# Sparse attention with a squared-ReLU FFN on one core: queries and choices transposed together by DMA

## The chip, the cores and the metric

The kernel runs on one core of one Trainium2 chip. The metric is the device time of one execution in microseconds, taken over several runs. A core has five engines that run their own instruction queues: TensorE (PE: matmuls, and transposes as matmuls with an identity), VectorE (DVE), ScalarE (ACT), GpSimd (POOL) and SyncE (SP), which only issues DMAs here. [...] Matmuls write PSUM; VectorE and ScalarE bring results from there to SBUF.

## What is computed

Attention over batch 4, 8 heads, 768 positions of 64 dimensions, in which each query looks at the 6 best of its chunks of 32 keys, followed by an FFN over the 3072 tokens with a squared ReLU. Cut to what matters:

```python
k_chunks = k.reshape(B, H, nc, chunk, D)            # chunk 32, nc 24
k_min, k_max = np.min(k_chunks, axis=3), np.max(k_chunks, axis=3)
ub = np.sum(np.maximum(q[:, :, :, None, :] * k_min[:, :, None, :, :],
                       q[:, :, :, None, :] * k_max[:, :, None, :, :]), axis=-1)
ub = np.where(causal, ub, -1000000000.0)            # by chunk
top_chunks = np.argsort(ub, axis=-1)[..., -top_k:]  # top_k 6
scores = scale * np.matmul(q, k.transpose(0, 1, 3, 2))
mask = sel & (pos[:, None] >= pos[None, :])         # sel: key's chunk is chosen
scores = np.where(mask, scores, -1000000000.0)
attn = np.exp(scores - np.max(scores, axis=-1, keepdims=True))
attn = attn / (np.sum(attn, axis=-1, keepdims=True) + 1e-09)
x = np.matmul(attn, v)                              # (B, S, H * D) = 3072 x 512
h = np.maximum(x @ w_in, 0.0)                       # 512 -> 2048
out = h * h @ w_out                                 # 2048 -> 512
```

## The kernel before

The work is cut into 8 half-blocks: half a batch, 384 queries, in the order `ORDER` (b0 first half, b1 first half, b0 second, b1 second, then b2 and b3, first half and second). A half-block has 4 slots `p`, one for each pair of heads; the 32 slots `s` run one after the other, and slot `s` is `p = s % 4` of half-block `hb = s // 4`. A first half (half 0) attends to 384 keys, a second half (half 1) to 768.

A slot's steps are written out by hand in one loop (a manual schedule: each engine executes its instructions in the order of the program text):

- `step_P`: the pair's keys and queries come with dimensions on the partitions. For the first three half-blocks TensorE transposes them (`step_T`) and they are placed in `kqs`; from half-block 3 (`ON_PE = 3`) on, DMA transposes bring a whole half-block (`tr`, one DMA of 4 blocks of 128x128 for each 128 tokens of k or q, into `kqT`), and `place_dma` copies keys and queries from there to `kqs`. `relus` makes relu(-q) and relu(q), `qr`.
- `step_K` (in six parts `k1`, one half-block ahead) or `extrema`: minimum and maximum of each chunk of keys, spread into `kbds`.
- `step_U`: TensorE makes the bounds `ub` of each query and chunk, VectorE takes the 8 best (`nc.vector.max`, six or four of them) and writes 1 for each chunk that is not chosen into `nsel`.
- `step_V`: TensorE transposes `nsel` (2 or 3 transposes a pair, one per 128 queries; L391), VectorE copies the result into `kqs` for each head (L395, L396).
- `step_E(s, hh, n)`: scores of one head. The matmul's operand in `kqs` has 128 rows: 64 dimensions of the head, and 64 rows of codes. On the key side a code row is -2^24 in the keys of one chunk (`oneh`), on the query side it is the transposed `nsel`: a chunk that is not chosen gets a score that exp turns to 0. Heads have the two groups of rows the other way round (`QROW`, `SROW`). ScalarE takes exp (L414), POOL masks the diagonal blocks (`affine_select`, L418) for `n == 1`. The scores have 3 PSUM buffers.
- `step_F(s)`, one slot later: attention times v, whose 65th column is 1 and gives the sum; VectorE divides (L443, L444) and writes `x`. At the end of a half-block, `step_X` transposes `x` to `xT`: on TensorE with `x_T` for the first two half-blocks and the last, by three DMA transposes (L484) for the others. Then the FFN of that half-block is queued.

The FFN is filler for TensorE. `fill` (in the loop `f1`) takes one piece from `queue`: an up-projection `ffn_up` (4 matmuls of 384 columns into `ph`, two buffers; ScalarE's relu, VectorE's square to `h`) or a quarter of a down-projection `ffn_down` (4 matmuls of 512 columns into `py`, one buffer; after the fourth quarter a copy to `ob` and a store by SP, L546 and L550). `quota` limits a slot to 6 to 8 pieces. The small uses of `psA` (`ub`, `qt`, `po` and others, tag "att") share two PSUM buffers.

Loads go out on POOL's queue (they convert to bf16), stores and DMA transposes on SP's. They are hung onto slots: `at(s, ...)` fills `later[s]`, and `go(s, 2)` and `go(s, 99)` issue two and then all of them, the first between the scores of head 0, the second behind `step_V`. `first[s]` is issued at a slot's start. k and q of half-block `g >= 4` load in slots `4g - 6` and `4g - 5`, are transposed in `4g - 5` and `4g - 3` and placed in `4g - 2`.

Of the kernel before, what the change touches and what calls it, by code (L numbers as in the profile page):

```python
# [39 lines left out]
def kernel(  # L40
# [30 lines left out]
    QROW = (D, 0)  # L71
    SROW = (0, D)

    kqs = [consts.tile([128, 2, NP, 4, HB], BF16, tag=f"kq{i}", name="kq") for i in range(2)]


    qn0 = consts.tile([128, HT, NP, 4, D], BF16, tag="qn0", name="qn")
# [3 lines left out]
    nsel = [consts.tile([128, HT, 2, D], BF16, tag=f"ns{i}", name="nsel") for i in range(3)]  # L81
# [28 lines left out]
    def load_q0(h):  # L110
        nc.gpsimd.dma_start(
            out=qn0[:, :, h // 2, 1 + h % 2, :],
            in_=q[0, h, 0:HB].rearrange("(j p) d -> p j d", p=128))
# [39 lines left out]
    for h in (6, 7):  # L153
        load_q0(h)

    oneh = consts.tile([D, S], BF16, tag="oneh")
    nc.vector.tensor_scalar_mul(
        oneh.rearrange("p (c j) -> p c j", j=CH),
        ident[0:D, 0:NC].unsqueeze(2).to_broadcast([D, NC, CH]), OFFSEL)

    def codes(i, half, copy, p0=0, p1=NP):
        for h in range(2):
            copy(kqs[i][SROW[h]:SROW[h] + D, h, p0:p1, 2 * half, :],
                 oneh[:, HB * half:HB * half + HB].unsqueeze(1)
                 .to_broadcast([D, p1 - p0, HB]))
# [22 lines left out]
    def blank(p0, p1, c):  # L188

        nc.scalar.mul(qn0[:, :, p0:p1, c, :],  # L190
                      ident[:, 0:D].unsqueeze(1).unsqueeze(1)
                      .to_broadcast([128, HT, p1 - p0, D]), 0.0)

    def clear():

        for h in range(2):
            nc.vector.memset(kqs[1][SROW[h]:SROW[h] + D, h, :, 1, 0:128], 0.0)
# [32 lines left out]
    def step_cast(n, p):  # L230
        if n == "k":
            nc.vector.tensor_copy(packed("k", 0)[:, 2 * p:2 * p + 2], staged["k", p])
        else:
            nc.scalar.copy(qn0[:, :, p, 1:3, :], staged["q", p])

    def step_T(s, kp, qp, ns="kq"):
# [3 lines left out]
        for n in ns:  # L240
            pool, tag = kp if n == "k" else qp
            x = t[n] = pool.tile([128, HB], BF16, tag=tag, name="t" + n)
            if n == "q" and s < NP:
                for j in range(HT):
                    nc.tensor.matmul(
                        x[:, 128 * j:128 * (j + 1)],
                        lhsT=qn0[:, j, p, 1:3, :].rearrange("p h d -> p (h d)"),
                        rhs=ident, is_transpose=True, start=True, stop=True)
# [26 lines left out]
    def place(s, n, copy, h0=0, h1=2):  # L275
        b, half, p = slots[s]
        for h in range(h0, h1):
            copy(by_token(kqs[b % 2][QROW[h]:QROW[h] + D, h, p, 2 * half + "kq".index(n), :]),
# [9 lines left out]
    def place_dma(g):  # L288
        b, half = ORDER[g]
        for h in range(2):  # L290
            nc.sync.dma_start(
                out=kqs[b % 2][QROW[h]:QROW[h] + D, h, :, 2 * half:2 * half + 2, :],
                in_=half_T(g)[D * h:D * h + D])
# [53 lines left out]
    def step_U(s):  # L347
        b, half, p = slots[s]
        ncs = 12 * (half + 1)
# [11 lines left out]
        for j in range(j0, HT):  # L361
# [3 lines left out]
            (qn0[:, j0:, p, 0:4:3, 0:ncs] if s < NP else nsel[s % 3][:, j0:, :, 0:ncs]),  # L365
# [3 lines left out]
    def qc(s, h):  # L369
        b, half, p = slots[s]  # L370
        return kqs[b % 2][:, h, p, 2 * half + 1, :]

    def step_V(s):
        b, half, p = slots[s]
        st[s]["e"] = [None, None]
        if s < NP:
            qt = psA.tile([128, 2, HB], BF16, tag="att", name="qt")
            for hh in range(2):
                for j in range(HT):
                    nc.tensor.matmul(  # L380
                        qt[:, hh, 128 * j:128 * (j + 1)],
                        lhsT=qn0[:, j, p, 2 * hh:2 * hh + 2, :]
                        .rearrange("p h d -> p (h d)"),
                        rhs=ident, is_transpose=True, start=True, stop=True)
            nc.vector.tensor_copy(kqs[b % 2][:, :, p, 2 * half + 1, :], qt)
# [4 lines left out]
        for j in range(j0, HT):  # L390
            nc.tensor.matmul(  # L391
                qt[:, 128 * j:128 * (j + 1)],
                lhsT=nsel[s % 3][:, j].rearrange("p h d -> p (h d)"),
                rhs=ident, is_transpose=True, start=True, stop=True)
        nc.vector.tensor_copy(qc(s, 0)[0:D, c:], qt[0:D, c:])  # L395
        nc.vector.tensor_copy(  # L396
            qc(s, 1)[D:128, c:], qt[D:128, c:])

    def step_E(s, hh, n):
# [7 lines left out]
        for (at, j, i0, m) in BANKS[half][n]:  # L407
# [3 lines left out]
                lhsT=kqs[b % 2][:, hh, p, 2 * (j // HT), 128 * (j % HT):128 * (j % HT + 1)],  # L411
# [12 lines left out]
    def step_F(s, hh):  # L424
# [13 lines left out]
        if hh == 1:  # L438
            if p == 0:
                xs[s // NP] = work.tile([128, HT, DM], BF16, tag="x", name="x")  # L440
# [4 lines left out]
                x[:, :, 128 * p:128 * (p + 1)].rearrange("p j (h d) -> p h j d", h=2),  # L445
                po[:, :, :, 0:D], r.to_broadcast([128, 2, HT, D]))
            st.pop(s)
# [14 lines left out]
    def x_T(hb, g, pt, us=(0, 1)):  # L462
# [3 lines left out]
        for u in us:  # L466
            for j in range(HT):
                nc.tensor.matmul(
                    pts[hb, g][:, u, 128 * j:128 * (j + 1)],
                    lhsT=xs[hb][:, j, 128 * (2 * g + u):128 * (2 * g + u + 1)],  # L470
# [5 lines left out]
    def step_X(hb, pe):  # L476
        xT = xT_of(hb)
# [4 lines left out]
        else:  # L482
            for j in range(HT):
                nc.sync.dma_start_transpose(  # L484
                    out=xT[:, :, 128 * j:128 * (j + 1)], in_=xs[hb][:, j, :])
# [17 lines left out]
    def ffn_last(hb):  # L503
# [3 lines left out]
        for g in range(2):  # L507
# [5 lines left out]
            ob = late.tile([128, DM], F32, tag="ob", bufs=3, name="ob")  # L513
            for c in range(2):
                (nc.scalar.copy if c else nc.vector.tensor_copy)(
                    ob[:, 128 * c:128 * c + 128], y[:, 128 * c:128 * c + 128])
                (nc.scalar if c else nc.sync).dma_start(
                    out[r0:r0 + 128, w * g + 128 * c:w * g + 128 * c + 128],
                    ob[:, 128 * c:128 * c + 128])
# [13 lines left out]
    def ffn_down(hb, py, t, c, act, tail):  # L533
# [9 lines left out]
        if c == 3:  # L543
            ob = late.tile([128, DM], F32, tag="ob", bufs=3, name="ob")
# [46 lines left out]
    for b in range(2, B):  # L591
        for g in range(2):
            at(8 * b - 2 + g, load_v, b, 4 * g, 4 * g + 4)
    for g in range(4, 2 * B):
        for i in range(2 * HT):
            at(4 * g - 6 + i // HT, load_n, "kq"[i // HT], g, i % HT)
    for g in range(ON_PE, 2 * B):
        s0 = 4 * g - 4 + (g == ON_PE)
        if g == ON_PE:
            for i in range(2 * HT):  # L600
# [225 lines left out]
```

## Time and profile before

| | |
|---|---|
| median of 3 runs | 278.2 us (277.95 to 281.56) |
| the profiled execution | 278.13 us, of which the span from the first to the last instruction is 276.4 us |
| granted TensorE clock, mean | 0.999 |
| DMA transposes (keys, queries, x) | 15 + 15 + 15, of 4 blocks each |
| transposes of choices on TensorE, L391 | 72 |
| fills: up-projections' matmuls, L524 | 512, 99.2 us busy |
| fills: down-projections' matmuls, L540 | 343 in the records, 83.9 us busy |
| masks on POOL, L418 | 64, 34.1 us busy, 138.2 us idle before them |

How to read the rows below. A row of a group of instructions has line, engine, operation, output and inputs, shapes, the count, then busy time, the mean ns of one, and the engine's idle time before them with what ended it. A matmul's duration has its way through the pipeline in it; two matmuls one behind the other start closer than that. Some matmul records are missing (L540 has 368 in the program). A row of waits reads: who waited, on whom, us in total, times, the longest. A row of a stretch has from:to, its length, then busy us and count of PE, PEld (weight loads), DVE, ACT and POOL, the granted clock, the DMA engines' share and GB/s.

### The profile page before, as it was taken

Reading aid. Unit: us, or ns where it says so; the run is one execution under the profiler, and the core shown is the slowest. Engines: PE = TensorE matmul, PEld = TensorE weight load, DVE = VectorE, ACT = ScalarE, POOL = GpSimd, SP = SyncE. Lnnn points to the kernel's source line nnn. Section 1 sums busy time; section 2 is a strip of 40 time slices with the busy share of each in tenths; the row PEclk is TensorE's granted clock in tenths of the full one; section 3 lists DMA queues with packets and bytes.
Section 4 is the critical chain, followed back from the end, with each engine's and each line's share of the span. In section 5 each row is a group of like instructions: output and inputs, shape, how many; then the busy total and the mean of one; then the engine's idle time right before and its main releaser. Section 6 shows DMA issues by size and latency. Waiting matters only on the chain.

```text
span 276.4 us, 6695 instructions
## 1 busy us (share of the span) xinstructions
PE 258.0 (93%) x2472; PEld 164.3 (59%) x2497; DVE 168.9 (61%) x647; ACT 181.9 (66%) x400; POOL 90.7 (33%) x135
## 2 busy tenths in 40 slices
PE   7887888899999999999999999999999999999994
PEld 6666555556666566655565566745565566655544
DVE  6878999666994368635884378615883455413411
ACT  5997879588975787835675777825674777625500
POOL 8695356316532017521551116701121111000000
PEclk9999999999999999999999999999999999999999
DMA  7999999959999259995699359997413200111002
GB/s 139 160 205 212 162 213 211 131 69 147 148 188 143 74 117 147 128 156 151 96 169 125 113 104 142 128 129 167 97 60 59 76 2 0 40 39 40 38 38 76
DMA packets 98272, 32.05 MB, mean 116 GB/s; under 512 B 84640, under 2 KB 93984, under 8 KB 98240
## 3 DMA queue, kind: packets, MB, share of 16 engines
q0 software_dynamic: 64688, 14.42, 66.6%
q1 hardware_dynamic: 32464, 16.88, 28.8%
q10 hardware_dynamic: 1088, 0.33, 0.5%
q8 instruction: 19, 0.31, 0.5%
q14 instruction: 13, 0.11, 0.1%
HBM read 27.26 MB, written 6.29 MB: 121 GB/s over the span
## 4 chain that ended last, share of the span: by engine, by line
PE 67%; DMA 9%; DVE 8%; ACT 7%; issue 3%; POOL 3%; SPq 1%; ACTq 0%; POOLq 0%; DVEq 0%
PE py L540 25%; PE ph L524 23%; PE ps L409 9%; PE po L434 7%; DMA vn<-in_v_dram 6%; ACT e L414 2%; ACT ht L528 2%; DVE h L530 2%; DMA xT<-x 2%; DVE km L321 1%; SPq L484 1%; DMA stage<-in_q_dram 1%; POOL e L418 1%; ACT ob L546 1%; PE ub L356 1%
## 5 line engine op out<-in xcount | busy, mean ns | idle before, releaser
L414 ACT ACTIVATE e<-ps 128x512 bf16<-128x512 f32 x192 | 97.1, 551 | 26.5 <-PE ps L409 26.5
L524 PE MATMUL ph<-xT,w_in 128*128 128x384 bf16 x512 | 99.2, 326 | 1.7 <-ACT ht L528 1.0
L540 PE MATMUL py<-w_out,h 128*128 128x512 bf16 x343 | 83.9, 379 | 2.6 <-ACT ob L546 0.9
L528 ACT ACTIVATE ht<-ph 128x384 bf16<-128x384 f32 x128 | 62.7, 500 | 27.5 <-PE ph L524 25.9
L418 POOL TENSOR_SCALAR_AFFINE_SELECT e<-e 128x384 bf16<-128x384 bf16 x64 | 34.1, 539 | 138.2 <-ACT e L414 138.2
L530 DVE TENSOR_TENSOR h<-ht 128x384 bf16<-128x384 bf16 x128 | 46.6, 376 | 43.9 <-ACT ht L528 43.6
L524 PEld LDWEIGHTS <-w_in 128*128 128x128 bf16 x512 | 47.5, 97 | 31.2 <-issue 2.4
L409 PE MATMUL ps<-kq 128*128 128x384 bf16 (+2 forms) x320 | 56.5, 278 | 1.8 <-DVE kq L395 0.8
L540 PEld LDWEIGHTS <-h 128*128 128x128 bf16 x368 | 34.9, 98 | 35.3 <-issue 1.7
L409 PEld LDWEIGHTS <-kq 128*128 128x128 bf16 x320 | 26.4, 98 | 14.5 <-issue 2.6
L434 PEld LDWEIGHTS <-e 128*128 128x128 bf16 x672 | 25.7, 98 | 6.7 <-issue 1.4
L363 DVE MAX8 m<-ub 128x8 f32<-128x24 f32 (+1 forms) x160 | 16.7, 171 | 20.3 <-PE ub L356 19.2
L434 PE MATMUL po<-vn,e 128*128 128x65 bf16 x672 | 27.1, 194 | 2.0 <-POOL e L418 0.8
L546 ACT COPY ob<-py 128x512 f32<-128x512 f32 x19 | 11.1, 586 | 22.7 <-PE py L540 22.3
L444 DVE TENSOR_TENSOR x<-po,r 128x384 bf16<-128x384 f32 x32 | 17.8, 558 | 1.1
L395 DVE COPY kq<-qt 64x384 bf16<-64x384 bf16 (+1 forms) x28 | 8.8, 315 | 12.4 <-PE qt L391 12.4
L105 POOL DMA_DIRECT2D kn<-in_k_dram x15 | 13.3, 891 | 0.6 <-DMA w_out<-in_moe_w_out_dram 0.4
L105 POOL DMA_DIRECT2D qn<-in_q_dram x15 | 13.3, 888 | 0.0
L321 DVE TENSOR_TENSOR km<-km 128x384 bf16<-128x384 bf16 (+3 forms) x40 | 11.3, 283 | 1.1
L356 PE MATMUL ub<-kbd,qr 128*128 128x48 bf16 (+1 forms) x160 | 9.5, 180 | 1.8 <-DVE kbd L219 0.8
L618 PE MATMUL idle<-ident 128*128 128x128 bf16 x97 | 8.7, 252 | 2.4 <-POOL ident masks.py:199 1.4
L121 POOL DMA_DIRECT2D vn<-in_v_dram x12 | 10.7, 904 | 0.4 <-issue 0.4
(68 smaller groups left out, 197.9 us busy)
## 6 DMA issues: line engine op xcount, KB each, us to landing
out_dram<-ob SPq DMA_DIRECT2D x23, 256.0 KB, 2.2
kq<-kqT SPq DMA_DIRECT2D x10, 384.0 KB, 5.2
w_in<-in_moe_w_in_dram POOLq DMA_DIRECT2D x2, 1024.0 KB, 13.2
w_out<-in_moe_w_out_dram POOLq DMA_DIRECT2D x2, 1024.0 KB, 19.7
kn<-in_k_dram POOLq DMA_DIRECT2D x15, 128.0 KB, 5.9
qn<-in_q_dram POOLq DMA_DIRECT2D x15, 128.0 KB, 7.0
vn<-in_v_dram POOLq DMA_DIRECT2D x12, 128.0 KB, 10.6
vn<-in_v_dram POOLq DMA_DIRECT2D x4, 384.0 KB, 7.8
```

The costliest lines, as they stand in the source:

```text
L105: nc.gpsimd.dma_start(out=nat_of(n, g)[:, DM * j:DM * j + DM].rearrange("p (h d) -> p h d", d=D), in_=rows(n, *ORDER[g], 0, H)[:, 128 * j: ...
L321: nc.vector.tensor_tensor(y, x[:, :, :, 0:m], x[:, :, :, m:2 * m], op=op)
L363: nc.vector.max(out=m8[:, j, hh, :], in_=ub[:, j - j0, hh, :])
L409: nc.tensor.matmul(ps[:, at:at + 128 * m], lhsT=kqs[b % 2][:, hh, p, 2 * (j // HT), 128 * (j % HT):128 * (j % HT + 1)], rhs=qc(s, hh)[:, c ...
L414: nc.scalar.activation(e[:, 512 * n + lo:512 * n + hi], ps[:, lo:hi], ACT.Exp, scale=float(scale))
L418: nc.gpsimd.affine_select(out=d, in_=d, compare_op=ALU.is_ge, fill=0.0, base=0, channel_multiplier=-1, pattern=[[0, 3], [1, 128]])
L434: nc.tensor.matmul(po[:, hh, i, :], lhsT=t["e"][hh][:, c:c + 128], rhs=vn[b % 2][:, 2 * p + hh, j, :], start=(j == 0), stop=(j == iq))
L444: nc.vector.tensor_mul(x[:, :, 128 * p:128 * (p + 1)].rearrange("p j (h d) -> p h j d", h=2), po[:, :, :, 0:D], r.to_broadcast([128, 2, HT ...
L524: nc.tensor.matmul(ph[:, 0:HB], lhsT=w_in[:, ki, 128 * f:128 * (f + 1)], rhs=xT[:, ki, :], start=(ki == 0), stop=(ki == NKI - 1))
L528: nc.scalar.activation(ht, ph[:, 0:HB], ACT.Relu)
L530: nc.vector.tensor_mul(h, ht, ht)
L540: nc.tensor.matmul(py[t], lhsT=h2[hb, f][:, 128 * t:128 * (t + 1)], rhs=w_out[:, f, :], start=(f == 0), stop=(f == NFI - 1))
```

## The change

Eight things are done together.

1. **Layout.** `kqs` has 96 rows in use instead of 128: 64 dimensions at the bottom and 32 code rows above them, for both heads alike (`KR = 96`); `qn0` and the codes follow. `step_T` of the first four slots transposes each head of a query pair by itself.
2. **Queries and choices together.** From half-block 3 on `step_U` writes the choices beside the queries of the pair, in `nsel`, where `step_Q` copies the queries on VectorE. `step_W` then transposes both with one DMA on SP's queue, 6 blocks, straight into `kqs`. `step_V` stays on TensorE for slots up to 12. `place_dma` copies keys alone.
3. **Order.** In half-blocks from 3 on `step_U` and `step_W` run two slots ahead instead of one, `step_P` and `step_Q` three slots ahead.
4. **x.** `x` is laid out by pairs, and each pair is transposed by its own DMA (3 blocks) as soon as `step_F` has made it; `step_X` no longer does it.
5. **Keys and queries sooner.** k and q of half-block `g` load in slots `4g - 8` and `4g - 7` (one later for `g = 4`), k is transposed in `4g - 6`, q in `4g - 4`, keys are placed in `4g - 3`; in the program these now stand behind `step_F`, so behind the x transposes. `step_K` starts a slot sooner.
6. **Loads behind selections.** In half-blocks from 3 on, all loads are issued behind the slot's last scores.
7. **Copies by halves.** The first of a half-block's three output tiles is copied from `py` in two halves, by VectorE and ScalarE, into tiles of their own, with a store each; `ob` has two buffers instead of three.
8. **Fills.** In half 0 some fills move from before the second head's scores to the slot's end. `x_T` of half-block 1 uses `ph`'s PSUM buffers.

```diff
-    kqs = [consts.tile([128, 2, NP, 4, HB], BF16, tag=f"kq{i}", name="kq") for i in range(2)]
+    CR = CH
+    KR = D + CR
+    kqs = [consts.tile([128, NP, 4, 2, HB], BF16, tag=f"kq{i}", name="kq") for i in range(2)]
...
+    chosen = [consts.tile([128, HT, 2, CR], BF16, tag=f"ch{i}", name="chosen")
+              for i in range(2)]
+    nsel = [consts.tile([128, 2, 2, HT, 2, D], BF16, tag=f"ns{i}", name="nsel")
+            for i in range(2)]
...
             if n == "q" and s < NP:
-                for j in range(HT):
-                    nc.tensor.matmul(
-                        x[:, 128 * j:128 * (j + 1)],
-                        lhsT=qn0[:, j, p, 1:3, :].rearrange("p h d -> p (h d)"),
-                        rhs=ident, is_transpose=True, start=True, stop=True)
+                for hh in range(2):
+                    for j in range(HT):
+                        nc.tensor.matmul(
+                            x[D * hh:D * hh + D, 128 * j:128 * (j + 1)],
+                            lhsT=qn0[:, j, p, hh, 0:D],
+                            rhs=ident, is_transpose=True, start=True, stop=True)
...
         for h in range(2):
             nc.sync.dma_start(
-                out=kqs[b % 2][QROW[h]:QROW[h] + D, h, :, 2 * half:2 * half + 2, :],
-                in_=half_T(g)[D * h:D * h + D])
+                out=kqs[b % 2][0:D, :, 2 * half, h, :],
+                in_=half_T(g)[D * h:D * h + D, :, 0, :])
...
+    def step_Q(s):
+        b, half, p = slots[s]
+        nc.vector.tensor_copy(
+            nsel[half][:, s % 2, :, :, 0, :],
+            nat["q", s // NP][:, 0:HT * DM]
+            .rearrange("r (j h d) -> r h j d", j=HT, h=H)[:, 2 * p:2 * p + 2])
+
+    def step_W(s):
+        b, half, p = slots[s]
+        nc.sync.dma_start_transpose(
+            out=kqs[b % 2][:, p, 2 * half + 1].rearrange("r h (j t) -> r (h j) t", j=HT),
+            in_=nsel[half][:, s % 2].rearrange("r h j n d -> r (h j n d)"))
...
-        if s < NP:
+        if s < NP or s // NP >= ON_PE:
...
+            if 2 <= s // NP < 2 * B - 1:
+                nc.sync.dma_start_transpose(
+                    out=xT_of(s // NP)[:, p, :].rearrange("r (j t) -> r j t", j=HT),
+                    in_=x[:, p].rearrange("p j t -> p (j t)"))
...
-        if c == 3:
-            ob = late.tile([128, DM], F32, tag="ob", bufs=3, name="ob")
+        if c == 3 and t == 0 and not tail:
+            w = DM // 2
+            r0 = S * ORDER[hb][0] + HB * ORDER[hb][1]
+            for g in range(2):
+                ob = late.tile([128, w], F32, tag=f"oh{g}", bufs=1, name="ob")
+                (nc.scalar.copy if g else nc.vector.tensor_copy)(
+                    ob, py[t][:, w * g:w * g + w])
+                nc.sync.dma_start(out[r0:r0 + 128, w * g:w * g + w], ob)
+        elif c == 3:
+            ob = late.tile([128, DM], F32, tag="ob", bufs=2, name="ob")
...
-            at(4 * g - 6 + i // HT, load_n, "kq"[i // HT], g, i % HT)
+            at(4 * g - (7 if g == 4 else 8) + i // HT, load_n, "kq"[i // HT], g, i % HT)
...
+    for g in range(ON_PE + 1, 2 * B):
         for j in range(HT):
-            at(s0 - 1, tr, g, "k", j)
-            at(s0 + 1, tr, g, "q", j)
-        at(s0 + 2, place_dma, g)
+            by_sp.setdefault(4 * g - (5 if g == 4 else 6), []).append((tr, g, "k", j))
+            by_sp.setdefault(4 * g - 4, []).append((tr, g, "q", j))
+        by_sp.setdefault(4 * g - 3, []).append((place_dma, g))
...
-            x_T(1, 0, A)
+            x_T(1, 0, F)
...
-        go(s, 2)
+        if hb < ON_PE:
+            go(s, 2)
         for n in range(hf, nb):
             step_E(s, 0, n)
...
-        if s + 1 < NS:
-            step_U(s + 1)
-        f1()
+        if s < NS - 2 or s + 1 == 3 * NP:
+            step_U(s + (1 if hb < ON_PE else 2))
+        if hb >= ON_PE and s < NS - 2:
+            step_W(s + 2)
...
+        late_f = half == 0 and hb > 2
+        if not (late_f and p in (0, NP - 1)):
+            f1()
         if p and s > NP:
             step_F(s - 1, 0)
             step_F(s - 1, 1)
-        if half == 0:
+        for fn, *a in by_sp.get(s, ()):
+            fn(*a)
+        if half == 0 and not (late_f and p in (0, NP - 1)):
             f1()
...
-        f1()
-        if s + 1 < NS:
+        if not (late_f and p == 0):
+            f1()
+        if hb < ON_PE:
             step_V(s + 1)
...
+        if s + 1 == ON_PE * NP:
+            f1()
+            step_Q(s + 2)
+            step_U(s + 2)
+            step_W(s + 2)
+        if hb >= ON_PE or s + 1 == ON_PE * NP:
+            if s + 3 < NS:
+                step_P(s + 3)
+                step_Q(s + 3)
```

125 lines of the change are left out of this document (65 added, 60 removed).

## The prediction

> **What bounds the kernel now.** I read the page first (engines, slices, chain), then TensorE's waits in the stretch that the change rewrites, then the rows of each operation that goes or comes.
>
> ```profile
> span 276.4 us, 6695 instructions
> ...
> PE 258.0 (93%) x2472; PEld 164.3 (59%) x2497; DVE 168.9 (61%) x647; ACT 181.9 (66%) x400; POOL 90.7 (33%) x135
> ...
> PE   7887888899999999999999999999999999999994
> ...
> PEclk9999999999999999999999999999999999999999
> ```
>
> ```profile
> PE 67%; DMA 9%; DVE 8%; ACT 7%; issue 3%; POOL 3%; SPq 1%; ACTq 0%; POOLq 0%; DVEq 0%
> ```
>
> TensorE is the bound: 93% of the span, nine tenths or more in every slice from the ninth to the last but one, at the full clock. From 109 us (slot 12, the first whose queries come by DMA transpose) to 242 us the stages can be taken as one:
>
> ```profile
> 109.00:242.00 133.00, 128.95 (x1182) 80.58 (x1196) 78.75 (x318) 87.37 (x190) 37.32 (x55) 1.00 0.87 103
> ```
>
> TensorE is busy for 128.95 of 133 us, ScalarE for 87, VectorE for 79. So time can be won here in two ways only: fewer matmuls, or fewer of TensorE's waits. All of its waits in that stretch:
>
> ```profile
> PE py L540 <- ACT ob L546: 0.9, 2, 0.5
> PE po L434 <- POOL e L418: 0.8, 2, 0.4
> PE ps L409 <- DVE kq L395: 0.6, 2, 0.3
> PE ph L524 <- DMA xT<-x: 0.6, 1, 0.6
> PE ub L356 <- DVE qr L301: 0.2, 1, 0.2
> ```
>
> They sum to 3.1 us in 8 waits. A wait costs more than its gap, because a row's duration has the pipeline's drain in it:
>
> ```profile
> L540 PE MATMUL py<-w_out,h 128*128 128x512 bf16 x343 | 83.9, 379 | 2.6 <-ACT ob L546 0.9 <-issue 0.2
> ```
>
> ```profile
> 262.56 6.91 PE py L540 x32
> 243.98 0.67 PE pt L468 x12
> ```
>
> The chain has 32 py matmuls in 6.91 us, 0.216 each, where the row's mean is 0.379: each wait also loses 0.379 - 0.216 = 0.16 us of overlap. With 8 x 0.16 = 1.3 us the waits of this stretch are worth 4.4 us.
>
> **Transposes that leave TensorE.** From slot 13 on, the transposes of the choices (L391) go; slot 12 has 6 where it had 3.
>
> ```profile
> L391 PE MATMUL qt<-ident,nsel 128*128 128x128 bf16 x72 | 8.6, 220 | 0.8 <-DVE nsel L364 0.8
> ```
>
> Of the 72, slots 4 to 11 keep 4 x 2 + 4 x 3 = 20, and slot 12 makes 6: 46 go. Against that, step_T of slots 0 to 3 transposes each head of a query pair by itself, 6 matmuls instead of 3: 12 come. Net 34 fewer. The chain above has 12 transposes in 0.67 us, 0.056 each: **-1.9 us**. They lie on the bounding engine, so the saving is not hidden; only the 12 in the first 20 us, where TensorE is not full, may cost less than their 0.67.
>
> With them go the copies behind them:
>
> ```profile
> L395 DVE COPY kq<-qt 64x384 bf16<-64x384 bf16 x16 | 5.5, 343 | 6.4 <-PE qt L391 6.4
> L396 DVE COPY kq<-qt 64x384 bf16<-64x384 bf16 x16 | 5.8, 361 | 0.5
> L302 DVE TENSOR_SCALAR qr<-kqT 128x384 bf16<-128x384 bf16 x12 | 3.0, 252 | 0.0
> ```
>
> 0.343 + 0.361 = 0.70 us of VectorE per slot of half 1. In their place step_Q copies 384 elements, nearest L302's 0.252 us. VectorE wins some 0.4 us a slot and was not the bound: nothing on the path, except that step_E no longer waits on the copies (below).
>
> **Waits that go.** Of the five rows: "ps <- kq" (0.6, 2) goes with the copies. "po <- e" (0.8, 2) is step_F of head 1 waiting on the mask after a single fill in a slot p = 3 of half 0; in the new order three up-projections stand there, 3 x 4 matmuls. "ub <- qr" (0.2) goes, since step_U now runs on relus of the slot before. "ph <- xT" (0.55) is the first up-projection of a half-block waiting on three transposes of 4 blocks each, begun after its last x. Now each x pair is transposed as it is made, so only one of 3 blocks is left after the last. Six waits, 0.6 + 0.8 + 0.2 + 0.55 = 2.15, and 6 x 0.16: **-3.1 us**.
>
> Slot 8's x_T moves from the pool that step_F also takes its po from to ph's pool:
>
> ```profile
> 50.43 0.53 PE L434 MATMUL po<-vn,e 128*128 128x65 bf16 x12 [0.65 <-DVE xT L474]
> ```
>
> 0.65 + 0.16: **-0.8 us**.
>
> **Copies by halves.** py has one buffer; the first tile's copy stands between its last matmul and the second tile's first, at 7 turns. Now VectorE copies one half and ScalarE the other. But in the changed instruction order ScalarE's half waits on VectorE's. The tail of before has such a pair already, and there ScalarE starts when VectorE is done:
>
> ```profile
> L546 ACT COPY ob<-py 128x512 f32<-128x512 f32 x19 | 11.1, 586 | 22.7 <-PE py L540 22.3
> L548 DVE COPY ob<-py 128x512 f32<-128x512 f32 x4 | 2.8, 692 | 8.7 <-PE py L540 8.7
> L515 DVE COPY ob<-py 128x128 f32<-128x128 f32 x2 | 0.6, 292 | 2.5 <-PE py L510 2.5
> L515 ACT COPY ob<-py 128x128 f32<-128x128 f32 x2 | 0.5, 266 | 10.0 <-DVE ob L515 8.5 <-DMA out_dram<-ob 1.5
> L414 ACT ACTIVATE e<-ps 128x256 bf16<-128x256 f32 x32 | 12.4, 389 | 2.1 <-PE ps L409 2.0
> ```
>
> 256 columns cost VectorE about 0.292 + (0.692 - 0.292)/3 = 0.43 us, ScalarE 0.389. One after the other that is 0.82 against 0.586, 0.23 more at each of the four turns in half 1 and at the last one. The two turns in half 0 get head 1's scores (128 + 384 + 256 columns, 0.32 us) as cover, and come out 0.1 better. Sum 5 x 0.23 - 0.2 = +0.95. If they run side by side after all: 0.586 - 0.43 = 0.16 less at each, -1.1. I take the row of the tail, **+0.9 us**.
>
> **What is added: W.** Nineteen step_W (slots 13 to 31), one DMA transpose of 6 blocks each, on SP's queue, for which these are the nearest rows:
>
> ```profile
> L305 SPq DMA_TRANSPOSE kqT<-qn x15: 1188/1219/1925, 66.0 to 191.6; - x15
> ...
> L291 SPq DMA_DIRECT2D kq<-kqT x10: 595/604/620, 76.0 to 196.7; - x10
> ...
> DMA to landing us min/median/max: 2.4/4.4/8.5
> ```
>
> Four blocks hold SP for 1.22 us; 6 hold it 1.22 (if the price is per instruction) to 1.83 us (if per block). A plain copy holds it for 0.60, so it is the blocks that cost, and I take 1.83; landing is then 2.4 + 0.61 = 3.0 us after issue in a quiet stretch and 8.5 + 0.6 = 9.1 in the worst. [...]
>
> What hides W: it is issued about where before's step_U of the next slot stood, and read by step_E two slots on. In the shortest slots:
>
> ```profile
> 129.22 0.19 PE L352 MATMUL ub<-cmask,ident 128*128 128x48 bf16 x1
> ...
> 140.12 0.38 PE L409 MATMUL ps<-kq 128*128 128x384 bf16 x2
> ```
>
> Between U's place and the reading scores lie 10.9 us, about 9.8 when VectorE's selection (some 1.1 us) is taken off. That covers 3.0, and just covers 9.1. Behind W on SP stand x's transposes, the next half-block's keys and queries, the k placements and the stores; per half-block 4 x 1.83 + 6 x 1.22 + 4 x 0.92 + 2 x 0.6 and about 1.7 of stores, 21 of some 30 us. step_Q of slot s + 3 waits on W of s + 1, as its buffer is free only then, and all of VectorE's queue stands behind it; the time to that point is also a slot and a half. Price taken: nothing.
>
> The loads are moved behind the masks on POOL's queue and two slots ahead. POOL is idle for two thirds, and a load holds it 0.9 us:
>
> ```profile
> L105 POOL DMA_DIRECT2D kn<-in_k_dram x15 | 13.3, 891 | 0.6 <-DMA w_out<-in_moe_w_out_dram 0.4
> ```
>
> Keys of half-block 4 now load in slot 9, behind three loads of v and two of codes: 3 x 0.9 more just before the queries' transposes of half-block 3, on which the first selections wait:
>
> ```profile
> 80.16 0.28 PE L356 MATMUL ub<-kbd,qr 128*128 128x48 bf16 x5 [0.55 <-DVE kbd L327]
> ```
>
> That wait can stay or grow by up to the 2.7 us of the loads. And step_U(13) now stands right behind U(12)'s slot, one up-projection (0.65) after slot 12's six transposes, whose copy and two relus VectorE makes first: about 0.5 us of new wait. I take **+0.5** for both, between 0 and 3.
>
> The scores' weights have 96 rows instead of 128. The only rows of such loads:
>
> ```profile
> L409 PEld LDWEIGHTS <-kq 128*128 128x128 bf16 x320 | 26.4, 98 | 14.5 <-issue 2.6 <-DVE kq L395 0.2
> L252 PEld LDWEIGHTS <-kn 96*64 96x64 bf16 x96 | 2.9, 113 | 2.2 <-issue 1.4 <-DVE kn L232 0.5
> ```
>
> 0.113 against 0.098: at most 320 x 0.015 = 4.8 us, if nothing covered it. Loads run beside the matmul before, so I take 0.
>
> Sum, against the profiled execution's 278.13 us (span 276.4 and 1.7 around it; the median of the three runs is 278.2, so no shift): -1.9 - 3.1 - 0.8 + 0.9 + 0.5 = -4.4, **273.7 us**.
>
> **Rivals.** *TensorE runs without waits.* All 8 waits of the stretch go (-4.4 for my -3.1), the halves run side by side (-1.1 for +0.9) and the 0.55 before U goes with its 0.16 (-0.7 for +0.5): 278.1 - 1.9 - 4.4 - 0.8 - 1.1 - 0.7 = 269.2. Any larger part of it is over 2% faster. For it: nothing but TensorE is above 70%. Against: ScalarE's half waits on VectorE's.
>
> *The gain is given back.* Two slots' worth of order is rewritten, and a wait that goes lets the next one show: of the 3.9 for waits only 1 is kept, and new ones come to 2 us: 278.1 - 1.9 - 1 + 0.9 + 2 = 278. For it: the gaps are all under 0.6 us, so covers of a single fill decide them.
>
> *W comes too late (slower).* Its place is the first scores of a slot in half 0, where the cover is 9.8 us. Before, transposes that ran beside a burst of loads took up to 8.5 us to land, and one was held in issue for 2.26 us:
>
> ```profile
> L484 SPq DMA_TRANSPOSE xT<-x x15: 1191/1261/2259, 86.9 to 211.9; - x15
> ```
>
> With both, 9.1 + 2.3 = 11.4, 1.6 us late; in the 8 slots of half 0 that is 13 us, 273.7 + 13 = 287. It decides from 9.8 us on. [...] Against: the new order has three loads of 128 KB, or one of v, in a slot, where before both stood together.
>
> **How the numbers follow.** My forecast (272.6 to 275.5) has 0.42, the run without waits 0.28, the gain given back (275.5 to 280) 0.18, a late W 0.12. The line at 2% (about what a measurement of this kernel can tell from no change) is 272.6 and 283.8 us: faster 0.29, same 0.59, slower 0.12. Range: from 270 (the lower third of the first rival left out) to 281, 8 in 10.
>
> **What would show it.** No L391 group but 26 transposes of choices; TensorE's rows "ps <- kq", "po <- e", "ph <- xT" gone after slot 12. ScalarE's half copy starting as VectorE's ends, and the py wait about 0.2 longer in half 1. W holding SP about 1.8 us and landing within 3 to 9. The prediction is wrong if step_E waits on a DMA, if VectorE waits on one before step_Q, or if another engine's busy share in the middle passes nine tenths.

## The result and the profile after

| | before | after |
|---|---|---|
| median us (6 runs each, taken together) | 278.56 (277.15 to 281.56) | 274.64 (274.51 to 276.55) |
| span of the profiled execution | 276.4 | 272.8 |
| ratio of the times | | 0.988, 95% interval 0.9841 to 0.9919 |

The change gains 1.2%: the interval ends below 1, but by the 2% line it counts as no change. In some runs of both kernels and of the experiments (six of the twelve of "Up-projections first", eight of the twelve of "As many bytes in other rows") the granted clock falls for some us, and they are 1 to 4 us longer (mean clock 0.987 to 0.994); where that could decide, the text goes by profiles.

The page of after, engines and chain:

```profile
span 272.8 us, 6680 instructions
...
PE 256.8 (94%) x2438; PEld 161.3 (59%) x2463; DVE 164.8 (60%) x635; ACT 178.3 (65%) x402; POOL 90.4 (33%) x135
...
PE 79%; DVE 12%; ACT 4%; issue 2%; DMA 1%; POOL 0%; ACTq 0%; DVEq 0%; POOLq 0%
```

TensorE has 34 instructions fewer. Its share of the chain went from 67 to 79%, mostly at the cost of DMA (9 to 1%) and POOL (3 to 0%), but that can't be put down to the change. The second profile of the same kernel, taken with the experiments, has before's shares:

```profile
PE 69%; DVE 9%; DMA 8%; ACT 7%; issue 3%; POOL 2%; SPq 0%; ACTq 0%; DVEq 0%; POOLq 0%
```

There, as in before, 6% of the chain are DMAs of values (`vn`), which land later than in the profile above. The stretch from 109 to 242 us, and TensorE's waits from 107 to 236 us:

```profile
109.00:242.00 133.00, 130.31 (x1163) 79.97 (x1177) 73.89 (x292) 87.42 (x193) 34.79 (x51) 1.00 0.88 113
```

```profile
PE py L565 <- ACT ob L573: 1.4, 4, 0.4
```

Five kinds of waits stood there before; one is left in this view, and it is that of the copies by halves. The view lists no wait below 0.15 us, and that matters below. A scale by slots tells where the time went: the mark of slot `s` is the start of the first matmul of `step_F(s)` (`po`), which runs one slot later, in us from the start of the span.

```
mark           before    after   difference
slot 4          34.30    33.68     -0.62
slot 8          64.30    62.81     -1.49
slot 13        105.89   106.17     +0.28
slot 31        239.40   235.37     -4.03
end of span    276.4    272.8      -3.6
```

Up to slot 8 after wins 1.5 us, in slots 8 to 13 it loses 1.8, and from there to slot 31 it wins 4.3. The loss in the middle has three places that waits show (TensorE's timeline of after):

```profile
83.28 0.47 PE L363 MATMUL ub<-kbd,qr 128*128 128x48 bf16 x6 [0.43 <-DVE qr L307]
...
105.45 0.22 PE L363 MATMUL ub<-kbd,qr 128*128 128x24 bf16 x3 [0.88 <-DVE kbd L333]
```

The first is step_U(13) on its relus, which VectorE makes directly ahead of it. The second is step_U(16): selections now run two slots ahead, and the last of the six parts `k1` of half-block 4's extrema stands directly ahead of it in slot 14, so that `kbd` isn't ready. The third is the py turn at about 90 us. At the price of 0.16 us of lost overlap for each wait (worked out in the prediction) the three are worth 0.43 + 0.88 + 0.33 + 3 x 0.16 = 2.1 us; before's wait in this part, 0.55 + 0.16 at 80.16, is gone. That leaves 1.4 of the 1.8.

From slot 13 to 31 the balance closes to 0.5 us: 43 transposes of choices fewer, 43 x 0.056 = 2.4 us; 8 waits of before, 3.1 + 1.3 = 4.4, against four of after, 1.4 + 0.6 = 2.0. That makes 4.8, measured 4.3.

### The profile page after: what moved, and what is told of

It reads as the page before. It is cut to its first block, busy times and chain, and to the rows that moved or that the text cites. A ratio compares the mean times of both kernels' runs of the same rounds, so it can differ in the third digit from the quotient of the medians.

```text
span 272.8 us, 6680 instructions
## 1 busy us (share of the span) xinstructions
PE 256.8 (94%) x2438; PEld 161.3 (59%) x2463; DVE 164.8 (60%) x635; ACT 178.3 (65%) x402; POOL 90.4 (33%) x135
## 4 chain that ended last, share of the span: by engine, by line
PE 79%; DVE 12%; ACT 4%; issue 2%; DMA 1%; POOL 0%; ACTq 0%; DVEq 0%; POOLq 0%
PE py L565 28%; PE ph L549 25%; PE ps L434 11%; PE po L460 7%; PE idle L650 3%; DVE h L555 2%; PE ub L363 2%; DVE km L327 2%; ACT e L440 1%; DVE kq L284 1%; DVE ob L573 1%; DVE m L370 1%; ACT ob L573 1%; DVE kq L410 1%; ACT ht L553 1%
## 5 line engine op out<-in xcount | busy, mean ns | idle before, releaser
L565 PE MATMUL py<-w_out,h 128*128 128x512 bf16 x343 | 82.8, 379 | 3.7 <-ACT ob L573 2.2
L434 PE MATMUL ps<-kq 96*128 96x384 bf16 (+2 forms) x320 | 56.4, 278 | 1.7 <-DVE kq L410 1.3
L434 PEld LDWEIGHTS <-kq 96*128 96x128 bf16 x320 | 26.5, 97 | 16.5 <-issue 1.7
L573 ACT COPY ob<-py 128x256 f32<-128x256 f32 x7 | 2.6, 373 | 21.1 <-DVE ob L573 21.1
L327 DVE TENSOR_TENSOR km<-km 128x384 bf16<-128x384 bf16 (+3 forms) x40 | 12.5, 313 | 1.0
L579 ACT COPY ob<-py 128x512 f32<-128x512 f32 x12 | 7.0, 586 | 9.2 <-PE py L565 8.8
L573 DVE COPY ob<-py 128x256 f32<-128x256 f32 x7 | 3.0, 425 | 16.2 <-PE py L565 16.2
L363 PEld LDWEIGHTS <-qr 128*128 128x128 bf16 x160 | 7.7, 96 | 5.7 <-DVE qr L307 1.7
```

Of the source, the lines that this page charges most:

```text
L327: nc.vector.tensor_tensor(y, x[:, :, :, 0:m], x[:, :, :, m:2 * m], op=op)
L363: nc.tensor.matmul(ub[:, j - j0], lhsT=st[s]["qr"][:, w, 128 * j:128 * (j + 1)], rhs=kbds[b % 2][:, p, w, :, 0:ncs], start=False, stop=(j ...
L434: nc.tensor.matmul(ps[:, at:at + 128 * m], lhsT=kqs[b % 2][0:KR, p, 2 * (j // HT), hh, 128 * (j % HT):128 * (j % HT + 1)], rhs=qc(s, hh)[: ...
L565: nc.tensor.matmul(py[t], lhsT=h2[hb, f][:, 128 * t:128 * (t + 1)], rhs=w_out[:, f, :], start=(f == 0), stop=(f == NFI - 1))
```

## Experiments

Each expectation was written before its run. Times are medians, ratios to the kernel before on the same chip. The changed kernel itself ran again beside the first three: 275.43 us, ratio 0.9876 (0.9843 to 0.991), with the same waits behind slot 8's mark and a new one ahead of it (attention on a load of values, 0.7 us).

**The copies by halves.** One edit, so that ScalarE copies the first tile whole:

```diff
-        if c == 3 and t == 0 and not tail:
+        if c == 3 and t < 0:
```

> The first output tile is copied whole by ScalarE again (as before the change), with two ob buffers. Theory (the halves run one after the other, 0.425 + 0.373 us, and hold py longer than one copy of 0.586): five turns get 0.21 back and the two in half 0, which have cover, almost nothing: 0.8 to 1.2 us faster than the changed kernel, about 273.6, and the waits of py's matmuls on ScalarE fall from 2.2 us to about 1. Rival (the halves shorten the turn or are covered): same or up to 1.1 us slower.

Measured: 273.35 us, 0.9812 (0.9775 to 0.9849), some 2 us below the changed kernel. What the halves did in after, on VectorE and ScalarE (rows of groups, then the timeline of one turn):

```profile
L573 DVE COPY ob<-py 128x256 f32<-128x256 f32 x7 | 3.0, 425 | 16.2 <-PE py L565 16.2
L573 ACT COPY ob<-py 128x256 f32<-128x256 f32 x7 | 2.6, 373 | 21.1 <-DVE ob L573 21.1
```

```profile
122.25 0.28 PE L434 MATMUL ps<-kq 96*128 96x256 bf16 x1
122.45 0.42 DVE L573 COPY ob<-py 128x256 f32<-128x256 f32 x1 [2.42 <-PE py L565]
122.49 0.49 PE L434 MATMUL ps<-kq 96*128 96x384 bf16 x3
122.91 0.37 ACT L573 COPY ob<-py 128x256 f32<-128x256 f32 x1 [3.26 <-DVE ob L573]
123.33 3.61 PE L565 MATMUL py<-w_out,h 128*128 128x512 bf16 x16 [0.35 <-ACT ob L573]
```

All of ScalarE's idle time before its half ends on VectorE's half, by a semaphore that the program waits for: 122.45 + 0.42 is 122.87, ScalarE starts at 122.91, and py's next matmul at 123.33. The scores between them cover some 0.5 us of the 0.80, and TensorE waits 0.25 to 0.35 us at each of the seven turns. With the whole copy, its row is:

```profile
L579 ACT COPY ob<-py 128x512 f32<-128x512 f32 x19 | 11.1, 585 | 27.3 <-PE py L565 18.7 <-issue 5.4 <-ACT e L440 2.9
```

0.585 us almost fits under the cover. No wait of py on a copy is listed any more, but py's matmul still starts right behind the copy: TensorE stands idle for 0.11 us at the two turns in half 0 and for 0.08 at those in half 1, where it was 0.35 and 0.32. So each of the first six turns wins 0.25 us, and so do the marks; the last wins 0.37. With everything else of the change in place, the halves cost 2 us. The expectation had 0.8 to 1.2, because it took the two turns in half 0 for covered.

**The late extrema.** One more `k1()` at the end of slot 13:

```diff
-        if hb == ON_PE - 1:
+        if hb == ON_PE - 1 or s == ON_PE * NP + 1:
             k1()
```

> One more part of the keys' minima and maxima of half-block 4 is made at the end of slot 13, so that all six are done before slot 14's bounds. Theory (the wait of 0.88 us at 105 us, ub on kbd, is lost time on TensorE, as VectorE makes the last part just before): 0.9 to 1.0 us faster than the changed kernel, about 273.6, and no such wait. Rival (TensorE has slack there, or the wait moves to the next step): same time, with a new wait behind it.

Measured: 274.32 us, 0.984 (0.9807 to 0.9872). The wait on `kbd` is gone from the trace, but at the same place there is a new one, as the rival had it:

```profile
105.16 0.24 PE L363 MATMUL ub<-kbd,qr 128*128 128x24 bf16 x3 [0.36 <-DVE qr L308]
```

From slot 12's mark to slot 13's it is 7.37 us, where after has 7.87: half of the 1.04 us is won here. The time alone can't tell 1 us from nothing beside after's own two medians; the combination below does.

**Up-projections first.** In the filler's order one up-projection stands ahead of the four down-projections and of the tile's turn:

```diff
-        for c in ("u" * NFI) if hb == 0 else "dddd" + "uuud" * 4 + "uuuu":
+        for c in ("u" * NFI) if hb == 0 else "dddd" + "uuud" * 4 + "uuuu" if hb == 2 * B - 1 else "udddd" + "uud" + "uuud" * 3 + "uuuu":
```

> In the queue of half-blocks 1 to 6 one up-projection (4 matmuls, 0.65 us) stands ahead of the second output tile's first quarter instead of behind its last. Theory (py's one buffer makes TensorE wait 0.3 to 0.35 us, and lose 0.16 more, at each turn between the first two tiles): six of the seven waits go, 6 x 0.49 = 2.9 us; the up-projection needs the last x pair's transpose 3.8 us after its attention, which may take back up to 0.4 at each: 1 to 2.9 us faster than the changed kernel, 271.7 to 273.6. Rival (the waits only move to xT): waits of ph on xT of 0.3 or more appear at the same places and the time is the same.

Measured: 276.63 us, 0.9945 (0.9908 to 0.9982): slower than the changed kernel, against the expectation, and with the waits that the rival named. The turns have their cover, and py waits only once more, for 0.3 us. But the four down-projections had been the cover of x's last transpose: ph waits on x three times, for 4.2 us together. TensorE's timeline, and stretches of 2 us (the granted clock stands behind POOL's busy time and count):

```profile
126.20 0.48 PE L549 MATMUL ph<-xT,w_in 128*128 128x384 bf16 x1 [2.08 <-DMA xT<-x]
126.47 5.14 PE L565 MATMUL py<-w_out,h 128*128 128x512 bf16 x16
...
187.43 0.32 PE L549 MATMUL ph<-xT,w_in 128*128 128x384 bf16 x1 [1.28 <-DMA xT<-x]
```

```profile
124.00:126.00 2.00, 0.12 (x1) 0.00 (x0) 1.86 (x8) 0.98 (x3) 1.31 (x3) 1.00 0.99 156
126.00:128.00 2.00, 1.80 (x5) 0.69 (x5) 1.45 (x6) 0.49 (x1) 2.00 (x3) 0.54 0.89 155
128.00:130.00 2.00, 2.00 (x7) 0.74 (x6) 0.12 (x1) 0.00 (x0) 0.38 (x1) 0.61 1.86 137
130.00:132.00 2.00, 2.00 (x12) 0.97 (x11) 0.00 (x0) 0.35 (x1) 0.00 (x0) 1.00 2.50 131
```

Behind the wait of 2.08 us the clock was 0.54 and 0.61 in two stretches of 2 us (by these, 1.7 us of clock lost in 4), and 16 matmuls took 5.14 us, where 16 of them took 3.61 in after (at 123.33 us). Here the wait cost its gap and 1.5 us more. Behind the wait of 1.28 us the clock stayed at 1.00.

**Choices back on TensorE.** W is left out, and for slots from 13 on `step_V` transposes queries and choices of a pair together, six matmuls a slot:

```diff
-        if hb >= ON_PE and s < NS - 2:
-            step_W(s + 2)
...
-        if hb < ON_PE:
+        if s + 1 < NS:
             step_V(s + 1)
...
             step_U(s + 2)
-            step_W(s + 2)
```

> The changed kernel's order, but queries and choices of slots 13 to 31 are transposed on TensorE (6 matmuls a slot) and copied by VectorE (0.54 us); the 19 DMA transposes of them go. Theory (TensorE is the bound, each transpose on it costs 0.056 us, and those DMAs are hidden): 19 x 6 x 0.056 = 6.4 us slower than the changed kernel, 280 to 282, more where scores wait on the copy. Rival (the DMA transposes are on the path, or TensorE has slack): within 2 us of the changed kernel or faster.

Measured: 281.07 us, 1.0087 (1.0058 to 1.0115). After's and this kernel's transposes:

```profile
L404 PE MATMUL qt<-ident,nsel 128*96 128x128 bf16 x6 | 0.5, 219 | 0.0
```

```profile
L404 PE MATMUL qt<-ident,nsel 128*96 128x128 bf16 x120 | 10.0, 219 | 0.0
```

114 more, 114 x 0.056 = 6.4 us by the price of the prediction, and 0.021 x 278.6 = 5.9 us measured, with some waits traded: two waits of scores on VectorE's copies (0.8 us) are back behind slot 13. The price holds. The new layout needs W: with the transposes of queries and choices on TensorE it is 0.9% slower than before.

**W one slot later.** `step_W(s + 1)` instead of `step_W(s + 2)`, everything else in its place (the early call at the end of slot 11 goes with it):

```diff
-        if hb >= ON_PE and s < NS - 2:
-            step_W(s + 2)
+        if hb >= ON_PE and s < NS - 1:
+            step_W(s + 1)
...
             step_U(s + 2)
-            step_W(s + 2)
```

> The DMA transpose of queries and choices is issued one slot later, so that its cover shrinks from some 9.8 us by a slot (6 to 9 us) to 1 to 4 us, against 2.7 to 5.6 us to landing. Theory (hidden only because of the two slots): scores wait on it, 0 to 3 us in each of 19 slots, together 10 to 35 us slower than the changed kernel, 285 to 310. Rival (the cover is far larger than counted, and the margin is not what matters): under 2 us.

Measured: 282.61 us, 1.0145 (1.0082 to 1.0208). The waits come, but at 7 of 19 places and for less than the 10 to 35 us expected. TensorE's timeline, three of the seven:

```profile
112.02 0.61 PE L434 MATMUL ps<-kq 96*128 96x384 bf16 x4 [0.88 <-DMA kq<-nsel]
120.45 0.39 PE L434 MATMUL ps<-kq 96*128 96x384 bf16 x2 [0.45 <-DMA kq<-nsel]
...
144.34 0.38 PE L434 MATMUL ps<-kq 96*128 96x384 bf16 x2 [1.75 <-DMA kq<-nsel]
```

The W that the scores at 112.02 wait for was issued at 103.06, held SP for 2.18 us and landed 8.92 us after issue; the 12 that nobody waited for landed within 2.7 to 4.4 us. So a landing of 9 us, the worst that the prediction reckoned with, does occur. The cover, from W's issue to the scores that read it, is 8.0 to 12.5 us in after, where no landing takes more than 5.6; here it is 2.9 to 8.1 (10.7 in the last slot), and the waits are where the landing is longer than the cover. With one slot less, seven waits of 6.7 us make the kernel 7 us slower than after.

**Twice the codes.** The loads of codes in slots 0 and 4 are issued twice, to the same place:

```diff
     at(0, codes, 1, 0, nc.gpsimd.dma_start)
+    at(0, codes, 1, 0, nc.gpsimd.dma_start)
...
+    at(4, codes, 0, 1, nc.gpsimd.dma_start)
     at(4, codes, 0, 1, nc.gpsimd.dma_start)
```

> The two loads of codes in slots 0 and 4 are issued twice, so that as many bytes of codes move in the first 45 us as before the change. Theory (the 1.2 us that the changed kernel gains in slots 0 to 7 beyond the forecast come from v's first loads landing 2.6 us sooner, as half the bytes of codes move ahead of them): v lands later again, attention waits on it by 0.3 to 0.7 us, and 0.5 to 1.3 us are lost, about 275.5. Rival (the early gain comes from the engines, from ScalarE's and VectorE's shorter work): under 0.3 us.

Measured: 292.36 us, 1.0488 (1.0434 to 1.0541), and nothing of what was asked. The second load writes what the first writes and waits for it on POOL; the masks stand behind it (timelines of POOL and of TensorE):

```profile
46.56 0.55 POOL L167 DMA_DIRECT2D kq<-oneh  x1 [12.42 <-DMA kq<-oneh]
```

```profile
48.26 0.51 PE L460 MATMUL po<-vn,e 128*128 128x65 bf16 x6 [9.55 <-POOL e L444]
```

TensorE stands for 9.55 us, and then runs slowly. Stretches of 6 us:

```profile
40.00:46.00 6.00, 0.00 (x0) 0.00 (x0) 0.06 (x1) 0.00 (x0) 0.00 (x0) 0.62 0.86 162
46.00:52.00 6.00, 2.84 (x20) 1.58 (x20) 0.75 (x2) 0.50 (x2) 3.52 (x6) 0.50 0.47 70
52.00:58.00 6.00, 6.00 (x59) 3.63 (x58) 5.00 (x18) 4.85 (x12) 3.52 (x5) 0.74 1.43 175
```

The clock is at 0.50 from 46 to 52 us. The run says nothing of bytes.

**As many bytes in other rows.** The same question without that wait: the code loads on POOL also write rows 96 to 127, which nothing reads.

```diff
-        for h in range(2):
-            copy(kqs[i][D:KR, p0:p1, 2 * half, h, :],
+        for r0, h in ((D, 0), (D, 1), (KR, 0), (KR, 1))[:4 if copy == nc.gpsimd.dma_start else 2]:
+            copy(kqs[i][r0:r0 + CR, p0:p1, 2 * half, h, :],
```

> The three loads of codes on POOL's queue (slots 0, 4 and 9) also write rows 96 to 127, which nothing reads: as many bytes as before the change, in four DMAs where the change has two. Theory: the halved codes let the values of the first slots land sooner, which gave most of the gain up to slot 7; here vn lands 1.5 to 2.6 us later, po waits for it, and the time is 276 to 277.5 us. Rival: the values land sooner because of the order of the loads; then only the POOL queue's issues come (0.9 us each, under its idle time), vn lands as in the changed kernel, and the time is 274.8 to 275.6.

Measured: 279.03 us, 0.9988 (0.9953 to 1.0023); the profile, at full clock, has 276.88 us. The last load of values lands at 34.11 us, in after at 32.47. But in the second profile of the changed kernel, with nothing edited, it lands at 35.07: from run to run this load moves by more than what was asked for, and the question on the bytes stays open. So does the premise of both experiments, the 2.6 us between before (35.09) and after. What shows is POOL's queue. Behind the two code loads that after has there too, three issues (the two added ones and one of `w_out`) each wait for a load of values; the last goes out at 34.40, where after's goes out at 29.73. The mask stands behind them, po waits 0.99 us on it, and slot 4's mark is 35.89, where it is 33.68 to 34.19 in nine profiles of kernels that are the same up to there.

**Fills of half 0 as before.** `late_f = False`:

```diff
-        late_f = half == 0 and hb > 2
+        late_f = False
```

> The fills of half 0 stand where they stood before the change (none moved to the slot's end). Theory (the two waits of attention on the mask, 0.40 each and 0.16 of overlap, went because three up-projections now stand ahead of it; the first tile's turn has cover from head 1's scores): the two waits come back and the turn's cover goes, 1 to 2 us slower than the changed kernel, about 276. Rival (those waits went for another reason): same.

Measured: 276.93 us, 0.9953 (0.9924 to 0.9983). TensorE's timeline, waits in half 0:

```profile
123.91 1.89 PE L565 MATMUL py<-w_out,h 128*128 128x512 bf16 x8 [0.69 <-ACT ob L573]
146.62 0.36 PE L460 MATMUL po<-vn,e 128*128 128x65 bf16 x6 [0.57 <-POOL e L444]
...
206.59 0.36 PE L460 MATMUL po<-vn,e 128*128 128x65 bf16 x6 [0.57 <-POOL e L444]
```

The two waits of po on the masks are back, at the places where before had them, and the turns in half 0 wait 0.69 instead of 0.35: the scores' cover is worth 0.34 us at each. Moving fills to the slot's end is what removed "po <- e".

**x transposed together.** The four transposes of a half-block's x stand behind the last pair:

```diff
-            if 2 <= s // NP < 2 * B - 1:
+            if p == NP - 1 and 2 <= s // NP < 2 * B - 1:
+              for pp in range(NP):
...
```

> The four x transposes of a half-block are issued together behind the last pair (half-blocks 2 to 6). Theory (the prediction's term): the last lands 3 x 1.2 us later, behind the cover of the four down-projections, and the first up-projections wait on it, 0.5 to 2 us at some of the five places: 275.9 to 279 us. Rival: the first up-projection reads nothing that the cover doesn't hide, and the waits that went with the change went for another reason: 275.0 to 275.6.

Measured: 275.05 us, 0.9888 (0.9843 to 0.9934), and no wait of ph on x: a miss. SP's timeline:

```profile
176.02 1.25 SPq L393 DMA_TRANSPOSE kq<-nsel  x1
177.37 6.30 SPq L475 DMA_TRANSPOSE xT<-x  x4
184.83 0.81 SPq L576 DMA_DIRECT2D out_dram<-ob  x2
```

The single starts are 177.37, 178.62, 179.96 and 182.46: SP came to them before the last pair's x was there (181.49), and had started three by then. The last landed at 186.50, and the first up-projection came at 188.71. At the first of the five places all four start about when the last x is ready (89.19), from 89.06 to 92.96; the last lands at 95.29, and the up-projection comes at 97.35, again without a wait. So the cover is longer than four transposes behind one another, and the wait stays away without transposing each pair as soon as it is made. What removed it stays open: the loads beside the transposes moved too, and a version with the old layout wasn't tried.

**x_T of half-block 1 in po's pool, as before:**

```diff
-            x_T(1, 0, F)
+            x_T(1, 0, A)
...
-            x_T(1, 1, F)
+            x_T(1, 1, A)
```

> The transposes of x of half-block 1, in slot 8, use the pool of po again, as before the change. Theory (the prediction's term): po waits 0.65 us on their copy, and the time is 0.8 us above the changed kernel's 275.4, 276.0 to 276.4. Rival: in the new order another buffer is free at that point, or ph's buffers were the dearer ones; 275.0 to 275.6, with no wait of po in slot 8.

Measured: 275.85 us, 0.9922 (0.9884 to 0.9959). TensorE's timeline:

```profile
50.67 0.53 PE L460 MATMUL po<-vn,e 128*128 128x65 bf16 x12 [0.65 <-DVE xT L504]
```

The wait of before is back to the hundredth. Between the marks of slots 6 and 7 this kernel loses 0.81 us on the changed one.

**Whole copy and earlier extrema together**, the two edits of the first two experiments:

> First tile copied whole, and one more part of the keys' extrema at the end of slot 13. Theory: the two waits have different places and their gains add: 2.0 + 0.6 to 1.1 below the changed kernel's 275.4, so 272.3 to 272.9 us, with no wait of py on a copy and none of U(16) on kbd. Rival: they share TensorE's time (what one wins, the next wait takes back): 273.2 to 273.6.

Measured: 272.39 us, ratio 0.979 (0.9738 to 0.9842), the fastest kernel of this study. Its stretch from 109 to 242 us:

```profile
109.00:242.00 133.00, 131.65 (x1169) 80.52 (x1183) 71.09 (x285) 87.96 (x191) 34.02 (x50) 1.00 0.92 113
```

TensorE is busy for 131.65 of 133 us, 1.3 more than in after. From slot 12's mark to slot 13's it is 1.02 us shorter than in the changed kernel's second profile, and the wait on `kbd` with its overlap is 0.88 + 0.16 = 1.04; the wait on relus that the late extrema alone brought up is not there. The two gains add.

## Why the prediction came out as it did

The time, 274.64, lies 0.9 us above the forecast of 273.7 and inside its range. The sum came out nearly right, but not all of its terms did, and chance has a part in it. By its steps:

- *Transposes, -1.9.* Right. Of the choices' 72 there are 26 left (6 in the row of L404 above, 20 at L416), and 114 of them brought back cost 5.9 us. Whether the 12 that come in slots 0 to 3 cost their 0.67 isn't shown: after is 0.47 us ahead at slot 3's mark (24.01 and 24.47), but in profiles of kernels that are the same that far the mark lies between 24.00 and 24.52.
- *Six waits that go, -3.1.* Five went, one didn't. "po <- e" went by the moved fills, as the step says, and comes back without them. "ps <- kq" went with the copies. "ph <- xT" went, but the reason given, each pair transposed as it is made, isn't needed for it: it stays away with all four behind the last pair. "ub <- qr" did not go. The step that failed is "goes, since step_U now runs on relus of the slot before": at the same place the bounds still wait on relus, too briefly for the view of waits. Before, then after:

```profile
135.28 0.19 PE L352 MATMUL ub<-cmask,ident 128*128 128x48 bf16 x1
135.69 0.30 PE L356 MATMUL ub<-kbd,qr 128*128 128x24 bf16 x4 [0.22 <-DVE qr L301]
```

```profile
134.57 0.23 PE L359 MATMUL ub<-cmask,ident 128*128 128x144 bf16 x1
134.94 0.46 PE L363 MATMUL ub<-kbd,qr 128*128 128x48 bf16 x6
```

  From start to start it was 0.41 us and is 0.37. Between the marks of slots 13 and 31 such waits, with their lost overlap, cost 0.60 us before and 0.83 after.
- *x_T to another pool, -0.8.* Right, 0.81 when undone.
- *Copies by halves, +0.9.* Right, mechanism and size. ScalarE's half starts as VectorE's ends (0.425 + 0.373 us against 0.43 + 0.389). From before to after TensorE's idle time goes from 0.08 to 0.32 us at the four turns in half 1 (+0.24, predicted +0.23) and from 0.45 to 0.35 at the two in half 0 ("0.1 better"); from slot 31's mark to the end, with the last turn, it is 0.37 longer. Together that is +1.1. The 2 us of the first experiment is another quantity: the halves alone, with the scores' cover in place. That cover, 0.34 us at each turn in half 0, comes from the moved fills, not from the halves.
- *New waits, +0.5.* Too small: they come to +0.9. U(13)'s wait was put at about 0.5 and is 0.43. The other, 0.88 us of U(16) on `kbd` in slot 14, was missing: the step looked at selections that now wait on relus and on queries, and not at the extrema, of which the last part stands directly ahead of the selection that reads it. Before's wait at 80.16, which was to stay or grow, went. With 0.16 for each, 0.6 + 1.0 - 0.7 = 0.9.
- *W, nothing.* Right, and it was a real condition: no engine waits on W. Its rows:

```profile
L393 SPq DMA_TRANSPOSE kq<-nsel x19: 1215/1218/2551, 87.1 to 217.9; - x19
...
DMA to landing us min/median/max: 2.7/2.8/5.6
```

  The price by blocks, 1.83 us of SP, was wrong: 6 blocks hold SP for 1.22 us as 4 do. The rival of a late W had the mechanism right: one slot later brings it about. The shortest cover is 8.0 us, not the 9.8 reckoned.
- *96-row weights, nothing.* Right: 97 ns a load after, 98 before.

```profile
L434 PEld LDWEIGHTS <-kq 96*128 96x128 bf16 x320 | 26.5, 97 | 16.5 <-issue 1.7 <-DVE kq L421 0.2
```

From slot 8's mark to the end the two profiles of the changed kernel are 2.2 and 2.1 us shorter than before. The measured sizes give more: 46 transposes -2.6, five waits -2.8, the relus +0.2, six turns +0.9, U(13) +0.6, U(16) +1.0, the wait at 80.16 -0.7, together -3.4. The missing 1.0 us is in waits below 0.15 us, which show only from start to start of TensorE's matmuls: bounds on relus at 78 and 83 us (three of 0.14), transposes of choices and the scores behind them at 65 and 73 us (four of 0.09), and two up-projections (0.09 each).

Ahead of slot 8's mark after wins 1.5 us and its second profile 0.5; the sum has 0.8 for x_T there, less one turn. In six profiles at full clock of kernels that are the same that far, the mark lies between 62.81 and 63.83 us (after has the lowest); before has one profile, 64.30. The last load of values shows where such a difference can come from: it lands at 32.47 us in after and at 35.07 in its second profile, and there attention waits 0.7 us on it. So up to 1 us of the gain before slot 8, and of the nearness of the forecast, may be chance, and what moves those landings stays open.

## What to carry to other kernels

Splitting a copy over two engines cost 2 us here, as the halves ran one behind the other (0.43 and 0.37 us, against 0.585 for the whole); look in the trace for a pair that already exists before paying for two. When a step is moved earlier by a slot, list all that it reads, each with the slot in which it is made: one input that keeps its old place takes back the gain. A wait that has left the view of waits may only have become shorter than the view lists: compare starts. Before an early gain is put down to a change, look at a second profile of the same kernel. On an engine that is full to 97%, what covers a wait is a named piece of work, and moving that piece (the four down-projections, the fills at the slot's end) uncovers the next wait.

## What the runs showed of the hardware

**A gap of 2 us on TensorE cost 3.6.** The rows of the third experiment show a gap of 2.08 us and then a clock of 0.54 and 0.61 in two stretches of 2 us; after gaps of 1.28 us there, and of 1.75 us with W one slot later, the clock stayed at 1.00. But the length of one gap doesn't settle it. In the profile of "x transposed together" the clock fell at about 20.6 us (0.90 in the first stretch, 0.50 in the second), in the second of two gaps of only 0.65 and 0.84 us, with TensorE busy for 0.79 of 2 us (the granted clock stands behind POOL's busy time and count):

```profile
19.00:21.00 2.00, 0.79 (x11) 0.43 (x10) 1.10 (x3) 1.05 (x3) 1.73 (x3) 0.90 1.11 197
21.00:23.00 2.00, 1.97 (x24) 1.69 (x25) 0.45 (x2) 1.18 (x3) 1.58 (x3) 0.50 1.13 214
```

**A DMA transpose from SBUF to SBUF held SP for 1.2 us, with 3, 4 or 6 blocks.** 3 blocks of x 1.198 us, 4 of keys or queries 1.227 and 1.225, 6 of W 1.218 (medians of after):

```profile
L474 SPq DMA_TRANSPOSE xT<-x x20: 1177/1198/2185, 64.8 to 205.7; - x20
```

```profile
L311 SPq DMA_TRANSPOSE kqT<-kn x15: 1205/1227/2087, 60.3 to 172.0; - x15
L311 SPq DMA_TRANSPOSE kqT<-qn x15: 1216/1225/2087, 66.1 to 186.8; - x15
```

By the block that is 0.40, 0.31 and 0.20 us, so fewer and larger transposes took less of SP here: at the median, W's nineteen come to 23 us of its queue instead of the 35 that the prediction's price by blocks gives.
